# Reordering the first block of a fused attention and gated-MLP kernel: v tile by tile, q and k in one piece, norm work re-timed

## The chip, the cores and the metric

One core of a Trainium2 chip. The metric is the device time of one execution in microseconds (us). The profile names the engines PE (TensorE matmuls), PEld (TensorE weight loads), DVE (VectorE), ACT (ScalarE), POOL (GpSimd) and SP (the queue that issues transfers). Times inside a trace count from the start of the span; the span is 1.7 to 2 us shorter than the time of the same execution. L562 is line 562 of that kernel, so line numbers differ between kernels.

## The reference, cut to what matters

```python
# S = 2048 rows, D = 448, 16 heads of 28, F = 1792, all bf16
xn = layernorm(x)                                   # per row, eps 1e-5
q, k, v = split_heads(xn @ wqkv)                    # wqkv 448 x 1344
scores = q @ k.T / sqrt(28), causal, window of 256 rows
attn = softmax(scores) @ v @ wo
mlp  = (gelu(xn @ w_gate) * (xn @ w_up)) @ w_down
out  = x + attn + mlp
```

The 2048 rows are worked in four blocks of 512, each of four tiles of 128 rows. Block 0 is tiles 0 to 3, block 1 is tiles 4 to 7. 448 is three full groups of 128 contraction rows and a rest of 64. A projection is therefore three dense matmuls and one of 64 rows, and two such 64-row matmuls can run side by side on two halves of the array (in the trace of the kernel before, those of q and k both start at 10.38 us).

## The kernel before: the parts that matter

Norm, the transposing transfer, and the banks of PSUM that the projections take in turn:

```python
def norm(t):                       # VectorE: 448 columns, then the last 64 again
    xn = work.tile([P, 4, P], bf16, name="xn", bufs=4)
    for eng, lo, n, src in ((nc.vector, 0, D, 0), (nc.vector, D, 64, 384)):
        eng.tensor_scalar(out=xf[:, lo:lo + n], in0=x_sb[:, t, src:src + n], ...)
def dma_transp(t):                 # tiles 4 and up: transposed by a transfer
    nc.sync.dma_start_transpose(out=xnT[:, :, t * P:(t + 1) * P], in_=...)

ring = [("m", "m", "d"), 0]        # banks m (two buffers) and d, in turn
def bank(name):
    tag = ring[0][ring[1] % len(ring[0])]
    ring[1] += 1
    return psum.tile([P, QB], f32, name=name, tag=tag, bufs=2 if tag == "m" else 1)
```

The order of block 0, and what the three first score steps carry along for block 1 (`aux`, one entry per score step):

```python
    norm(2)
    norm(3)
    run(gen_v(0, (0,)))                       # v of tiles 0 and 1, own 64-row pair
    qk = gen_qk(0, (0,), 0, 2 * P)            # q and k of group 0, first half of the rows
    next(qk)
    transp(2, 1, nc.scalar.copy, "o")
    transp(3, 1, nc.vector.tensor_copy, "m")
    ...
    run(gen_qk(0, (0,), 2 * P, 2 * P))        # second half of the rows
    rstd(4, 2)
    ...
    aux = [lambda: rstd(6, 2), lambda: (norm(6), norm(7), loads()), lambda: None] ...
```

Of the kernel before, what the change touches and what calls it, by code (L numbers as in the profile page):

```python
# [12 lines left out]
f32 = mybir.dt.float32  # L13
i32 = mybir.dt.int32

S, D, H, Dh, F = 2048, 448, 16, 28, 1792
P = 128
NT = S // P
NF = F // P
# [56 lines left out]
def kernel(  # L76
# [21 lines left out]
    def score_pool(n):  # L98

        if phase[0] is not None:  # L100
            phase[0].close()
        phase[0] = ExitStack()
        phase[0].pool = phase[0].enter_context(tc.tile_pool(name="sps", bufs=n, space=bass.MemoryType.PSUM))

    score_pool(1)
    xv = A_x.rearrange("b (n p) d -> p (b n) d", p=P)
    outv = out.rearrange("b (n p) d -> p (b n) d", p=P)

# [12 lines left out]
    def rows(w, c0, n):  # L121
        return w[c0 * P:(c0 + n) * P, :].rearrange("(c p) n -> p c n", p=P)

    nc.sync.dma_start(out=x_sb[:, 0, :], in_=xv[:, 0, :])
    nc.scalar.dma_start(out=x_sb[:, 1, :], in_=xv[:, 1, :])
    nc.sync.dma_start(out=x_sb[:, 2:4, :], in_=xv[:, 2:4, :])
    nc.sync.dma_start(out=wv[:, 0:3, :], in_=rows(A_wqkv, 0, 3)[:, :, 2 * D:3 * D])
    nc.scalar.dma_start(out=wraw[:, 0:3, :], in_=rows(A_wqkv, 0, 3)[:, :, 0:2 * D])
    for a in range(2):
        nc.sync.dma_start(out=wv[64 * a:64 * a + 64, 3, :], in_=A_wqkv[384:448, 2 * D:3 * D])  # L130
    for a in range(2):
        nc.sync.dma_start(out=wraw[64 * a:64 * a + 64, 3, 0:D], in_=A_wqkv[384:448, a * D:(a + 1) * D])
    nc.sync.dma_start(out=x_sb[:, 4:8, :], in_=xv[:, 4:8, :])

    ident = const.tile([P, P], bf16, name="ident")
    make_identity(nc, ident[:, :])
# [16 lines left out]
                        nc.gpsimd.affine_select(out=m, in_=m, pattern=[[kind, 64]], compare_op=ALU.is_ge, fill=0.0,  # L153
                                                base=min(kind, 0), channel_multiplier=-kind)

    make_masks()

    eps_t = const.tile([P, 1], f32, name="eps_t")
    nc.vector.memset(eps_t[:, :], 1e-5)
# [15 lines left out]
    l_all = const.tile([P, NB * 4, 16], f32, name="l_all")  # L175

    def warmup(n):
        wps = phase[0].pool.tile([P, 4, QB], f32, name="wps", tag="s")
        for i in range(n):
            nc.tensor.matmul(wps[:, i % 4, :], lhsT=warm[:, 0:P], rhs=warm[:, 0:QB], start=True, stop=True)  # L180


    def stat(t):
# [11 lines left out]
    def norm(t):  # L195
        xn = work.tile([P, 4, P], bf16, name="xn", bufs=4)
        xf = xn[:, :, :].rearrange("p a b -> p (a b)")
        for eng, lo, n, src in ((nc.vector, 0, D, 0), (nc.vector, D, 64, 384)):
            eng.tensor_scalar(out=xf[:, lo:lo + n], in0=x_sb[:, t, src:src + n], scalar1=mv_all[:, t, 0:1],
                              scalar2=rstd_all[:, t:t + 1], op0=ALU.subtract, op1=ALU.mult)  # L200
        xns[t] = xn
# [27 lines left out]
# [4 lines that stand above are left out]
        return psum.tile([P, QB], f32, name=name, tag=tag, bufs=2 if tag == "m" else 1)  # L233


    def gen_v(qb, ts):

        for t in ts:
            pvs = []
            for i in range(2):  # L240
                pv = bank("pv")
                cs = slice((t + i) * P, (t + i + 1) * P)
                mm3(pv[:, 0:D], lambda c: xnT[:, c, cs], lambda c: wv[:, c, :], True, False)
                pvs.append(pv)
                yield (570, HOLD) if i else 570
            for i in range(2):
                mm_half(pvs[i][:, 0:D], xnT[:, 3, (t + i) * P:(t + i + 1) * P], wv[:, 3, :], i, False, True)
            for i in range(2):
                (nc.vector.tensor_copy if qb > 1 or i else nc.scalar.copy)(out=v_sb[:, t + i, :, 0:Dh], in_=pvs[i][:, 0:D].rearrange("p (h d) -> p h d", d=Dh))
            yield -360  # L250

    def gen_qk(qb, gs, lo=0, n=QB):

        ts = slice(qb * QB + lo, qb * QB + lo + n)
        for g in gs:
            hs = slice(4 * g, 4 * g + 4)
            pq = bank("pq")
            mm3(pq[:, 0:n], lambda c: wqp[:, c, hs, :].rearrange("p h d -> p (h d)"), lambda c: xnT[:, c, ts], True, False)
            yield 650
            pk = bank("pk")  # L260
            mm3(pk[:, 0:n], lambda c: wkp[:, c, hs, :].rearrange("p h d -> p (h d)"), lambda c: xnT[:, c, ts], True, False)
            yield 650, HOLD
            w3 = w3p[:, hs, :].rearrange("p h d -> p (h d)")
            mm_half(pq[:, 0:n], w3, xnT[:, 3, ts], 0, False, True)
            mm_half(pk[:, 0:n], w3, xnT[:, 3, ts], 1, False, True)
            nc.scalar.copy(out=qT[:, g, ts], in_=pq[:, 0:n])  # L266
            nc.vector.tensor_copy(out=kT[:, g, ts], in_=pk[:, 0:n])  # L267
            if lo + n == QB:
                done.add((qb, g))
            yield -360  # L270

    def gen_proj(qb):
# [323 lines left out]
    def run(gen):  # L596
        for _ in gen:
            pass

    warmup(10)  # L600
    stat(0)
    rstd(0, 1)
    stat(1)
    rstd(1, 1)
    norm(0)
    transp(0, 1, nc.scalar.copy, "o")
    norm(1)
    warmup(1)
    transp(1, 1, nc.scalar.copy, "d")
    stat(2)  # L610
    stat(3)
    rstd(2, 2)
    pads(nc.vector.tensor_copy, wqp, slice(0, 1))
    nc.vector.tensor_copy(out=w3p[:, :, 0:Dh], in_=wraw[:, 3, 0:D].rearrange("p (h d) -> p h d", d=Dh))
    pads(nc.scalar.copy, wkp, slice(0, 1))
    norm(2)
    norm(3)
    run(gen_v(0, (0,)))
    qk = gen_qk(0, (0,), 0, 2 * P)
    next(qk)  # L620
    transp(2, 1, nc.scalar.copy, "o")
    transp(3, 1, nc.vector.tensor_copy, "m")
    stat(4)
    run(qk)
    stat(5)
    pads(nc.vector.tensor_copy, wqp, slice(1, 4))
    pads(nc.vector.tensor_copy, wkp, slice(1, 4))
    run(gen_qk(0, (0,), 2 * P, 2 * P))
    rstd(4, 2)
    stat(6)  # L630
    v23 = gen_v(0, (2,))
    next(v23)
    next(v23)
    norm(4)
    norm(5)
    stat(7)

    def loads():

        for t in range(4, 8):  # L640
            dma_transp(t)
        nc.sync.dma_start(out=wu[:, :, :], in_=rows(B_w_up, 0, 3))
        for t3, lo, hi in ((wgu3, B_w_gate, B_w_up), (wug3, B_w_up, B_w_gate)):
            nc.sync.dma_start(out=t3[0:64, :], in_=lo[384:448, :])
            nc.sync.dma_start(out=t3[64:128, :], in_=hi[384:448, :])
        for lo in (0, F // 2):
            nc.sync.dma_start(out=wg[:, :, lo:lo + F // 2], in_=rows(B_w_gate, 0, 3)[:, :, lo:lo + F // 2])
        wo_v = A_wo.rearrange("(g j d) n -> j d g n", g=4, j=4)
        for j in range(4):
            nc.sync.dma_start(out=wo[32 * j:32 * j + Dh, :, :], in_=wo_v[j])  # L650
        for k in range(0, NF, 3):
            n = min(3, NF - k)
            nc.sync.dma_start(out=wd[:, k:k + n, :], in_=rows(B_w_down, k, n))

    for qb in range(NB):
        early = ()
        aux, plan = [], {}
        if qb < 2:
            aux = [lambda: rstd(6, 2), lambda: (norm(6), norm(7), loads()), lambda: None] * (1 - qb) + [lambda t=t: stat(t) for t in range(8, 12)] * (1 - qb) + [lambda: rstd(4 * qb + 8, 4)]
        if qb == 0:  # L660
            new_hT(0)
            early = (2, 8)
            feeds = [Feed((v23, 360), (gen_qk(0, (1, 2, 3)), 3 * QK1), (gen_proj(1), PROJ), (gen_up(0, early), UP1 * len(early)))]
            feeds[0].held = True
        else:
            ring[0] = ("m",)
            tags = "dodo" if last_tag[0] == "o" else "odod"
            feeds = [Feed((gen_down(qb - 1, tags), DOWN))]
            if qb < 3:
                feeds.append(Feed((gen_proj(qb + 1), PROJ)))  # L670
                plan = {0: 1140, 1: 1140, 2: 1300, 4: 1300, 6: 1300, 7: 1300}
            else:
                new_hT(3)
                early = (2, 4, 6, 8, 10)
                feeds.append(Feed((gen_up(3, early), UP1 * len(early))))
                plan = {0: 1300, 2: 1300, 4: 1300, 6: 1300, 7: 1300}
        if qb:
            score_pool(1)
        rest, after = attention(qb, feeds, aux, plan)
        nc.scalar.preload_act_table(ACT.Gelu_apprx_tanh)  # L680
        score_pool(2)
        if qb not in hTs:
            new_hT(qb)

        def hook(f):
            after(f)
            if f >= 4 and qb < 2:
                t = 4 * qb + 4 + f // 2
                if f < 12:
                    norm(t + 2)  # L690
                    dma_transp(t + 2)
                    if qb == 0:
                        stat(t + 6)

        gated(qb, early, rest, hook)
        if qb < NB - 1:
            nc.scalar.preload_act_table_set("natural_log_exp_and_others")
# [138 lines left out]
```

## Time and profile before

| | kernel before |
|---|---|
| time, median of 3 runs | 227.72 us (227.51 to 228.32) |
| span of the profiled execution | 225.3 us |
| PE busy | 217.1 us |
| the first scores start | 13.29 us |
| the fourth score step starts | 20.07 us |
| v of tile 7 starts | 23.44 us |
| last weight load of the kernel | 220.16 us |

The front is everything up to the fourth score step; the prediction below shows its lines. Three groups of lines are needed later and are not in it. The first is VectorE's norms of tiles 6 and 7, and SP's issue of the last of the transposing transfers (start, length, engine, line, operation, out<-in):

```profile
16.70 1.42 DVE L199 TENSOR_SCALAR xn<-x_sb,mv_all,rstd_all 128x448 bf16<-128x448 bf16 x4
...
18.93 2.32 SPq L205 DMA_TRANSPOSE xnT<-xn  x1
```

The six matmuls are the v of tiles 6 and 7 without a gap:

```profile
22.86 1.31 PE L218 MATMUL pv<-wv,xnT 128*128 128x448 bf16 x6
```

```profile
42.93 1.27 DVE L380 TENSOR_TENSOR hT<-ge,u 128x512 bf16<-128x512 bf16 x2
...
43.87 0.37 PE L223 MATMUL u<-xnT,wgu 64*128 64x512 bf16 x1
```

### The profile page before, as it was taken

The numbers are of one execution on the slowest core, as the hardware profiler recorded it, in microseconds if no ns is written. First come the engines' busy times: TensorE is split into PE (matmuls) and PEld (weight loads), VectorE is DVE, ScalarE is ACT, GpSimd is POOL, SyncE is SP. The second block draws the span as 40 slices with busy tenths as digits, with TensorE's granted clock in tenths as the row PEclk, the third lists the DMA queues.
The fourth block names the chain that finished last, engine by engine and source line by source line (L and its number), as shares of the span: only waits on it lengthen the run. The fifth ranks groups of instructions, "written<-read, shape, count | busy, mean of one in ns | idle before, by whom it ended". The sixth has DMA issues, their size and how long they took to land.

```text
span 225.3 us, 5435 instructions
## 1 busy us (share of the span) xinstructions
PE 217.1 (96%) x2262; PEld 97.0 (43%) x2262; DVE 147.6 (66%) x353; ACT 133.3 (59%) x129; POOL 43.4 (19%) x63
## 2 busy tenths in 40 slices
PE   6899999999999999999999999999999999999991
PEld 2533333344444444444444445444344435344571
DVE  5996887768675647588555666596345776679320
ACT  4678897524878876422868886333576775664000
POOL 8514867220000002222000002222000002222000
PEclk9999999999999999999999999999999999999998
DMA  6916999311100101001300100000000000100011
GB/s 222 323 28 74 314 293 292 112 23 38 36 0 24 25 5 44 4 0 37 61 0 23 25 3 25 23 0 0 0 4 20 25 5 5 43 3 0 22 42 29
DMA packets 18454, 12.69 MB, mean 56 GB/s; under 512 B 9784, under 2 KB 17784, under 8 KB 18424
## 3 DMA queue, kind: packets, MB, share of 16 engines
q1 hardware_dynamic: 17880, 11.48, 19.4%
q10 hardware_dynamic: 544, 0.80, 1.0%
q8 instruction: 19, 0.31, 0.6%
q14 instruction: 11, 0.09, 0.1%
HBM read 8.77 MB, written 1.84 MB: 47 GB/s over the span
## 4 chain that ended last, share of the span: by engine, by line
PE 87%; DVE 4%; ACT 3%; DMA 1%; POOL 1%; issue 0%; DVEq 0%
PE po L301 19%; PE gt L218 16%; PE u L218 12%; PE po L296 6%; PE sc L539 6%; PE gt L223 5%; PE ov L501 4%; PE ue L218 4%; PE pq L218 4%; PE pk L218 4%; PE pv L218 4%; PE pq L223 2%; ACT p_sb L543 1%; DMA x_sb<-in_A_x_dram 1%; POOL oN L451 1%; PE ue L223 1%
## 5 line engine op out<-in xcount | busy, mean ns | idle before, releaser
L543 ACT ACTIVATE p_sb<-sc 128x2048 bf16<-128x2048 f32 (+2 forms) x42 | 73.9, 1759 | 10.2 <-PE sc L539 8.5
L301 PE MATMUL po<-wd,hT 128*128 128x448 bf16 (+1 forms) x238 | 50.0, 342 | 0.0
L376 ACT ACTIVATE ge<-gt 128x1024 bf16<-128x1024 f32 x28 | 28.7, 1024 | 35.4 <-PE u L223 22.2
L218 PE MATMUL gt<-xnT,wg 128*128 128x512 bf16 x168 | 40.5, 380 | 0.0
L451 POOL TENSOR_TENSOR oN<-oc,rb 128x512 bf16<-128x512 f32 x10 | 12.7, 1268 | 118.0 <-DVE ri L480 62.1
L380 DVE TENSOR_TENSOR hT<-ge,u 128x512 bf16<-128x512 bf16 x42 | 26.9, 682 | 11.8 <-ACT ge L376 11.7
L218 PE MATMUL u<-xnT,wu 128*128 128x512 bf16 x126 | 30.6, 379 | 0.0
L301 PEld LDWEIGHTS <-hT 128*128 128x128 bf16 x238 | 21.6, 98 | 18.6 <-issue 2.2
L432 DVE TENSOR_TENSOR p_sb<-p_sb,masks 128x256 bf16<-128x256 bf16 (+1 forms) x90 | 24.6, 329 | 0.0
L218 PEld LDWEIGHTS <-wg 128*128 128x128 bf16 x168 | 15.1, 98 | 21.6 <-issue 5.4
L218 PEld LDWEIGHTS <-wu 128*128 128x128 bf16 x168 | 16.0, 98 | 19.2 <-issue 1.0
L507 DVE TENSOR_TENSOR oc<-oc,ov 128x512 f32<-128x512 f32 x12 | 8.3, 688 | 19.4 <-ACT oc L506 19.4
L539 PE MATMUL sc<-qT,kT 32*64 32x320 bf16 (+7 forms) x640 | 16.9, 263 | 0.5 <-ACT p_sb L543 0.3
L306 DVE TENSOR_TENSOR res<-po,x_sb 128x448 bf16<-128x448 f32 (+1 forms) x17 | 9.9, 585 | 10.4 <-PE po L301 10.1
L442 POOL TENSOR_SCALAR_AFFINE_SELECT p_sb<-p_sb 128x512 bf16<-128x512 bf16 (+1 forms) x20 | 14.2, 730 | 12.7 <-ACT p_sb L543 12.7
L296 PE MATMUL po<-wo,oN 128*128 128x448 bf16 (+1 forms) x68 | 16.3, 343 | 0.0
L267 DVE CAST kT<-pk 128x512 bf16<-128x512 f32 (+1 forms) x17 | 11.0, 649 | 7.9 <-PE pk L223 7.9
L506 ACT COPY oc<-ov 128x512 f32<-128x512 f32 x12 | 7.0, 585 | 15.2 <-POOL oN L451 12.8
L451 POOL TENSOR_TENSOR oN<-oc,l 128x512 bf16<-128x512 f32 x6 | 8.4, 1395 | 30.7 <-DVE l L468 30.7
L335 DVE CAST hT<-ue 128x512 bf16<-128x512 f32 x14 | 9.0, 686 | 7.1 <-PE ue L223 7.1
L223 PE MATMUL gt<-xnT,wgu 64*128 64x512 bf16 x49 | 13.6, 380 | 0.1
L266 ACT CAST qT<-pq 128x512 bf16<-128x512 f32 (+1 forms) x17 | 9.5, 558 | 6.6 <-PE pk L223 6.6
(75 smaller groups left out, 240.3 us busy)
## 6 DMA issues: line engine op xcount, KB each, us to landing
out_dram<-res SPq DMA_DIRECT2D x15, 112.0 KB, 1.9
wu<-in_B_w_up_dram SPq DMA_DIRECT2D x1, 1344.0 KB
wg<-in_B_w_gate_dram SPq DMA_DIRECT2D x2, 672.0 KB, 10.4
wd<-in_B_w_down_dram SPq DMA_DIRECT2D x4, 336.0 KB, 8.1
x_sb<-in_A_x_dram SPq DMA_DIRECT2D x1, 896.0 KB, 6.0
wraw<-in_A_wqkv_dram ACTq DMA_DIRECT2D x1, 672.0 KB, 4.8
x_sb<-in_A_x_dram SPq DMA_DIRECT2D x1, 448.0 KB
wo<-in_A_wo_dram SPq DMA_DIRECT2D x4, 98.0 KB
```

What stands on the lines that cost most here:

```text
L218: nc.tensor.matmul(ps, lhsT=lhs(c), rhs=rhs(c), start=start and c == 0, stop=stop and c == 2, skip_group_check=True)
L223: nc.tensor.matmul(ps, lhsT=lhs[p0:p0 + 64], rhs=rhs[p0:p0 + 64], start=start, stop=stop, tile_position=(p0, 0), skip_group_check=True)
L267: nc.vector.tensor_copy(out=kT[:, g, ts], in_=pk[:, 0:n])
L296: nc.tensor.matmul(po[:, 0:w], lhsT=oN[:, g, cs], rhs=wo[:, g, lo:up], start=(g == 0), stop=False, skip_group_check=True)
L301: nc.tensor.matmul(po[:, 0:w], lhsT=hT[:, f, cs], rhs=wd[:, f, lo:up], start=False, stop=(f == NF - 1), skip_group_check=True)
L376: nc.scalar.activation(out=ge[:, :, :], in_=pr["gt"][:, :, :], func=ACT.Gelu_apprx_tanh)
L380: nc.vector.tensor_tensor(out=hT[:, f + i, :], in0=ge[:, i, :], in1=u[:, :], op=ALU.mult)
L432: nc.vector.tensor_tensor(out=reg, in0=reg, in1=m, op=ALU.mult)
L442: nc.gpsimd.affine_select(out=reg, in_=reg, pattern=mid + [[1 if diag else -1, min(w, P)]], compare_op=ALU.is_ge, fill=0.0, base=0 if diag ...
L451: nc.gpsimd.tensor_tensor(out=oN[:, g, :], in0=oc[:, :], in1=inv, op=ALU.mult)
L539: nc.tensor.matmul(ss[k0:k0 + nk, j, col:col + nq], lhsT=kT[r, g, kt * P + k0:kt * P + k0 + nk], rhs=qT[r, g, qb * QB + q0:qb * QB + q0 + ...
L543: nc.scalar.activation(out=p_sb[:, :, 0:ncol], in_=ss[:, :, 0:ncol], func=ACT.Exp, scale=SCALE)
```

## The change

Its intent is to start v of each tile as soon as that tile is transposed, to do q and k of group 0 once over 512 columns instead of twice over 256, and to put the 64-row rests of v beside those of q and k, so that PE changes its tiling less often. Norm work of block 1 moves behind the first scores. Cut to its core:

```diff
-    score_pool(1)
+    score_pool(2)                      # q and k of group 0 borrow score banks
...
-        for eng, lo, n, src in ((nc.vector, 0, D, 0), (nc.vector, D, 64, 384)):
+        for eng, lo, n, src in ((nc.vector, 0, D, 0), (nc.gpsimd if t in (1, 2) else nc.vector, D, 64, 384)):
...                                     # gen_qk(qb, gs, others):
+            qk_halves(qb, g, pq, pk)
+            for t, pv in others:       # 64-row rests of v of tiles 2 and 3
+                v_half(t, pv)
+            if others:
+                v_copy(*others[1], nc.vector.tensor_copy)
+            qk_copies(qb, g, pq, pk)
...
-    norm(3)
-    run(gen_v(0, (0,)))
-    qk = gen_qk(0, (0,), 0, 2 * P)
-    ...
+    v_dense(0, pvs[0])
+    norm(2)
+    pads(...)                          # two on VectorE, one on ScalarE
+    transp(2, 1, nc.scalar.copy, "o")
+    pvs.append(bank("pv")[:, 0:D])
+    v_dense(1, pvs[1])
+    norm(3)
+    make_masks()
+    transp(3, 1, nc.vector.tensor_copy, "d")
+    pvs.append(alone("pv", "o"))
+    v_dense(2, pvs[2])
+    proj(pq, wqp, 0, 0)
+    proj(pk, wkp, 0, 0)
+    ...
+    pvs.append(alone("pv", "d"))
+    v_dense(3, pvs[3])
+    ring[1] = 0
...
+    def ahead():
+        for t in (4, 5):
+            norm(t)
+            dma_transp(t)
+        stat(6)
+    def ahead2():
+        stat(7)
+        rstd(6, 2)
+        v_copy(2, pvs[2], nc.vector.tensor_copy)
...
-            aux = [lambda: rstd(6, 2), lambda: (norm(6), norm(7), loads()), lambda: None] ...
+            aux = [ahead, ahead2, lambda: (norm(6), norm(7), loads())] ...
```

Cut away: the q and k weights come in four transfers, the gate weights in one, and w_down in fewer.

## The prediction

> **What bounds the kernel now.** I read the page's first lines, then busy time in three stretches, then TensorE's timeline of the front, then the chain of waits there, then VectorE's timeline. The page gives a span of 225.3 us with PE busy for 217.1 us (96%). The stretches (columns: stretch, length, then busy us and instructions of PE, PE weight loads, DVE, ACT, POOL, then clock, DMA share, GB/s) say where the rest is:
>
> ```profile
> 1.96:7.14 5.18, 4.73 (x20) 2.06 (x21) 3.77 (x14) 2.91 (x7) 4.74 (x13) 1.00 1.03 341
> 7.14:20.07 12.93, 12.09 (x81) 5.31 (x81) 11.31 (x33) 9.47 (x18) 5.46 (x13) 1.00 0.49 134
> 20.07:221.30 201.23, 200.33 (x2165) 89.65 (x2163) 131.55 (x305) 120.70 (x105) 31.89 (x32) 1.00 0.17 45
> ```
>
> From 20.07 us, where the fourth score step starts, to the end of the last matmuls PE is busy for 200.33 of 201.23 us, and the list of waits has none for PE after 18 us. That long stretch follows the front rigidly. So this change can be worth only what moves the moment at which that fourth score step starts. Before it lie 1.96 us of start-up, 5.18 us of warm-up and first norms, and 12.93 us of projections of block 0.
>
> The timeline of PE there (start, length, instruction; matmul lengths contain latency, so I use start to start):
>
> ```profile
> 7.14 1.29 PE L218 MATMUL pv<-wv,xnT 128*128 128x448 bf16 x6 [0.45 <-DMA wv<-in_A_wqkv_dram]
> ...
> 9.00 0.73 PE L213 MATMUL tp<-ident,xn 128*128 128x128 bf16 x8
> 9.96 0.49 PE L218 MATMUL pk<-xnT,wkp 128*128 128x256 bf16 x3 [0.23 <-DVE v_sb L249]
> ...
> 15.76 0.34 PE L539 MATMUL sc<-qT,kT 32*128 32x384 bf16 x4 [0.34 <-ACT p_sb L543]
> 16.24 0.81 PE L218 MATMUL pq<-xnT,wqp 128*128 128x512 bf16 x3
> ...
> 18.35 0.82 PE L218 MATMUL pq<-xnT,wqp 128*128 128x512 bf16 x3
> 19.00 0.81 PE L218 MATMUL pk<-xnT,wkp 128*128 128x512 bf16 x3
> 19.75 0.39 PE L223 MATMUL pq<-xnT,w3p 64*128 64x512 bf16 x1
> ...
> 20.07 0.40 PE L539 MATMUL sc<-qT,kT 32*128 32x128 bf16 x8
> ```
>
> Work in 7.14 to 20.07, start to start: v of tiles 0 and 1 1.52 (7.14 to 8.66), q/k group 0 in two halves 2.13 (0.34, 0.63, 1.16), two transposes 0.73, v of tiles 2 and 3 1.54, score steps 0.33, 0.28 and 0.23, three later q/k groups 1.72, 1.71, 1.72. That is 11.91, so 1.02 us is waiting: 0.23 before k at 9.96, 0.42 before the second score step at 15.76, 0.20 before q at 16.24, and the rest around 18. The chain of waits (start, length, what) says on whom:
>
> ```profile
> 13.92 1.78 ACT p_sb L543
> ...
> 15.71 0.30 ACT lnv L190
> ...
> 16.04 0.20 ACT rstd_all L191
> 16.25 0.47 ACT qT L266
> 16.72 1.36 ACT p_sb L543
> ...
> 18.12 0.29 PE sc L539 x4
> ```
>
> The single score buffer makes step two wait for the first exp; then two small ACT operations of block 1's norm (the inverse deviations of tiles 6 and 7) stand before the q copy and push the second exp to 16.7. VectorE's timeline shows that it is just as late:
>
> ```profile
> 13.84 1.09 DVE L199 TENSOR_SCALAR xn<-x_sb,mv_all,rstd_all 128x448 bf16<-128x448 bf16 x4
> 14.84 0.62 DVE L185 BATCH_NORM_STATS2 st<-x_sb 128x6 f32<-128x448 bf16 x1
> 15.50 0.18 DVE L186 BATCH_NORM_AGGREGATE mv_all<-st 128x2 f32<-128x6 f32 x1
> 15.60 0.59 DVE L249 CAST v_sb<-pv 128x448 bf16<-128x448 f32 x1
> 16.11 0.68 DVE L267 CAST kT<-pk 128x512 bf16<-128x512 f32 x1
> ```
>
> The v copy at 15.60, behind two norms and a statistic of block 1, frees the bank that q at 16.24 needs (15.60 plus 0.59 is 16.19). VectorE is busy 4.70 and 4.90 us in the two 5 us stretches from 5 to 15. It is nearly a co-bound of the front, which decides my number.
>
> **What the Trainium skill says.** "TensorEngine Tiling (Array Packing)", Tiling Modes, Key Properties, says that changing the tiling mode drains TensorE. The trace agrees: q/k of one group takes 1.72 us, six dense matmuls and a concurrent pair of 64-row ones are 7 times 0.216 = 1.51 (0.65 for three, 16.24 to 16.89), so an excursion costs about 0.2 us; for v, 1.53 against 7 times 0.19 = 1.33 (448 of 512 columns), again 0.2. "TensorE: Matmul & The Clock Gate", Part 1, says that the array runs at half clock until about 3.4 us of sustained activity, in a window that runs free of the kernel. The trace agrees: the first warm-up weight loads take 152 ns and the last 98 ns, and the turn is near 5.6 us, some 3.6 us after 1.96. "SBUF — State Buffer", SBUF: two separate sides, says that VectorE's two-port modes and GpSimd share one port pair under an exclusive lock. The trace fits that: two norms took 1.0 us with POOL idle (13.84 to 14.84) and 1.39 us while POOL masked scores (16.70 to 18.09). "DMA: Bandwidth & Descriptors", Specifications, wants at least 512 B per descriptor; the new first pieces of the q and k weights have 224 B rows. No line of this trace prices those; I take them as twice their 168 KB.
>
> **The change, part by part.**
> 1. v tile by tile, q/k in one piece, last rows shared. Two half-width q/k groups (2.13) become one: 7 times 0.216 plus one excursion is 1.72, saving 0.41. The v of tiles 0 to 3 lose two excursions of their own, since their last rows ride in group 0's and group 1's: 3.06 becomes 4 times 0.57 plus two pairs of 0.19, or 2.66, saving 0.40. Work falls from 11.91 to about 11.1.
> 2. The q/k weights in four pieces (the heads of group 0 first) instead of one. Before, wv was on the path: PE waited 0.45 us for it at 7.14, behind 672 KB of q/k weights. Now 168 KB of them precede it, so at the 375 GB/s of that stretch I estimate it near 6.4. But a statistic now stands ahead of the second norm, which ends near 6.6 instead of 6.0 (0.65 us more on VectorE), and its transposes near 7.05. The first v starts at 7.05: gain 0.1.
> 3. My time table from there, with durations of this trace: third norm 7.35 to 7.75, transposes to 8.15, v of tile 1 to 8.75, transposes of tile 3 to 9.15, v of tile 2 to 9.75 (its copy on ACT, behind the fourth deviation and the k padding, is done near 9.1), q and k to 11.1, four half-row matmuls to 11.6, v of tile 3 to 12.3. Meanwhile the copies of q (ACT 0.57) and k (DVE 0.6) end near 12.1. So the first scores start at about 12.3 instead of 13.29. Gain here 1.0, of which 0.19 is owed for the last rows of tiles 2 and 3.
> 4. First exp 12.7 to 14.55 (1.88 before). q/k group 1 with the v rows ends near 14.4, the second scores run 14.6 to 14.9. So 0.42 us of waiting shrinks to about 0.15, and the two ACT operations of tiles 6 and 7 come after the second exp.
> 5. Then VectorE: k copy to 12.0, two small pads to 12.4, v of tile 1 to 12.9, two larger pads to 13.5, norms 4 and 5 to 14.5, one statistic to 15.25, v of tile 3 to 15.8. The next q needs that bank. PE is ready at 14.9, so a new wait of 0.9 us appears (0.20 before). The masks of POOL now run until about 13.3 (6.0 us from 7.2) beside those pads; allow 0.1 to 0.4 for the shared port. I take 15.9.
> 6. From there to the fourth scores: 0.65 and 1.07 for group 2, 0.3 scores, 1.72 group 3, as before, to about 19.65.
>
> Sum: 20.07 minus 19.65 is 0.4 us, of about 0.8 us less work and 1.0 us at the first scores; the rest is given back at the bank of step 5. 227.72 minus 0.4 is 227.3 us.
>
> What is off the path: fewer, larger loads of later weights (gate weights in one piece; they are read at 39.4, and 3.7 MB from 22.9 at 300 GB/s end near 35), eight warm-ups for ten, masks later (needed first in block 1), two 64-column norm tails on POOL.
>
> **The rivals.**
> - Without the VectorE wait. If the v copy comes by 14.9 (for it: one statistic, 0.75, and two tails less are ahead of it), PE has only 0.3 to 0.4 us of waits: 7.05 plus 11.1 plus 0.4 is 18.55, a gain of 1.5 and a time of 226.2. Against it: the k copy cannot start before the half rows end near 11.4, and the seven operations of step 5 then follow.
> - The start slips. The second norm comes later, the short rows load slowly, POOL's tails wait for the port, or eight warm-ups with a thinner sequel leave the array at half clock for another window. Every 0.5 us of delay at the first v is 0.5 us more; half clock over part of the v work some 1.5. Time 227.8 to 229. For it speaks that the turn to full clock came only near 5.6; against, that PE still has work from 1.96 to 6.2.
> - A later wait. Norms 6 and 7 now come after two v copies, some 1.1 us later (19.2 for 18.1). The transpose of tile 7 started moving 1.1 us after its issue and took 1.0, so it lands near 22.4; its v is due at 22.9. Another 1 us late on VectorE costs 0.5 us: 227.8.
>
> **Range and chances.** All waits gone gives 226.2, all gain lost and a slip gives 228; within, VectorE decides. 8 in 10: 226.4 to 228.0. Two per cent is 4.6 us, more than all waiting of the front, so faster by that has chance 0.01; slower by it would need the clock and a load to fail together, 0.02; within 0.97.
>
> **What would show it.** Right: the first scores near 12.3, second near 14.6; PE's longest wait after 10 us before group 2's q, put down to the v copy, near 1 us; fourth scores near 19.6; no PE waits afterwards. Wrong: the first v after 7.5; weight loads of 152 ns past 6.5 us; a wait at the v of tile 7 or at a gate matmul; or group 2's q starting right after the second scores.

## More of the kernel before

The gated part (its code and its lines at 43 us are in this section) takes up the turn of the banks where the attention left it, for its first pair only. The later pairs have a turn of their own between "d" and "o":

```python
def begin(f):                                  # f = 0, then pairs (2, 4), (6, 8), ...
    ...
    tags = (("m", 2), alone)                   # alone: "d" or "o", by turns
    if qb == 0 and f == 0:
        nxt = [ring[0][(ring[1] + i) % 3] for i in range(2)]
        tags = [(x, 2 if x == "m" else 1) for x in nxt]
```

## The result, and the profile after

| | before | after |
|---|---|---|
| time, median of 4 runs each | 227.95 us (227.51 to 228.32) | 228.74 us (228.45 to 228.87) |
| ratio after/before, fast runs | | 1.0034, 95% interval 1.0011 to 1.0056 |
| span of the profiled execution | 225.3 us | 227.0 us |
| PE busy | 217.1 us | 215.0 us |

Ratios here are the mean time of one kernel's fast runs over that of the other's fast runs of the same rounds, so they are not quite the ratio of the medians quoted. One execution of the kernel before, beside four of the experiments (from the v copy on ScalarE to the norm tails on VectorE), was slow (313.76 us at a clock of 0.658) and is left out.

The change is within 2%, as predicted, but on the other side: 0.8 us slower where 0.4 us faster was expected, and outside the range. PE shows 2.1 us less busy time and ends later. But 25 of the 2,252 matmul records are missing from this trace. In the repeat below, whose trace has them all, PE is busy for 217.0 us, so nearly all of the 2.1 us is missing records and not saved work. The stretches of the new kernel, with the columns as in the prediction, are these:

```profile
6.85:19.94 13.09, 11.52 (x75) 4.29 (x75) 12.04 (x34) 9.15 (x17) 8.66 (x25) 1.00 0.54 159
19.94:222.50 202.56, 198.75 (x2141) 89.42 (x2163) 131.52 (x305) 120.69 (x105) 32.12 (x32) 1.00 0.18 45
```

PE was busy for 200.33 of 201.23 us in the long stretch before. It now shows 198.75 of 202.56, with 22 records missing there. The repeat, with none missing, shows 200.64 of 202.14 (from 19.71 us): 1.50 us not busy for 0.90 before. (All three windows end 1.1 us behind the last weight load.) The front is ahead only by 0.13 us at its end, in this pair of profiles. PE's timeline there:

```profile
6.85 0.73 PE L221 MATMUL pv<-wv,xnT 128*128 128x448 bf16 x3
...
12.49 0.40 PE L562 MATMUL sc<-qT,kT 32*128 32x128 bf16 x8
...
16.28 0.81 PE L221 MATMUL pq<-xnT,wqp 128*128 128x512 bf16 x3 [1.02 <-DVE v_sb L246]
...
19.94 0.40 PE L562 MATMUL sc<-qT,kT 32*128 32x128 bf16 x8
```

The first scores come 0.80 us sooner than before. Then q of group 2 waits 1.02 us for VectorE's v copy, as foreseen. VectorE has the norms of tiles 4 and 5 and a statistic ahead of that copy, and then another statistic, another copy and a k copy ahead of the norms of tiles 6 and 7:

```profile
15.64 0.59 DVE L246 CAST v_sb<-pv 128x448 bf16<-128x448 f32 x1
16.15 0.68 DVE L274 CAST kT<-pk 128x512 bf16<-128x512 f32 x1
16.75 0.62 DVE L188 BATCH_NORM_STATS2 st<-x_sb 128x6 f32<-128x448 bf16 x1
...
17.49 0.59 DVE L246 CAST v_sb<-pv 128x448 bf16<-128x448 f32 x1
18.13 0.69 DVE L274 CAST kT<-pk 128x512 bf16<-128x512 f32 x1
18.74 1.11 DVE L202 TENSOR_SCALAR xn<-x_sb,mv_all,rstd_all 128x448 bf16<-128x448 bf16 x4
```

The norms that started at 16.70 now start at 18.74. SP's issues of the two transposing transfers that hang on them, the chain of waits there, and PE where it needs tile 7 (the kernel after):

```profile
19.36 2.17 SPq L208 DMA_TRANSPOSE xnT<-xn  x1
...
21.63 1.22 SPq L208 DMA_TRANSPOSE xnT<-xn  x1
```

```profile
21.63 2.42 DMA xnT<-xn
24.05 0.05 issue
```

```profile
24.10 0.74 PE L221 MATMUL pv<-wv,xnT 128*128 128x448 bf16 x3 [0.62 <-DMA xnT<-xn]
```

The first v of tile 7 starts 0.65 us later than before, 24.10 for 23.44. And in the gated part of block 0 a wait appears where there was none (VectorE's two multiplications, and the second 64-row matmul of the pair after):

```profile
43.50 1.28 DVE L403 TENSOR_TENSOR hT<-ge,u 128x512 bf16<-128x512 bf16 x2
```

```profile
44.83 0.37 PE L226 MATMUL u<-xnT,wgu 64*128 64x512 bf16 x1 [0.29 <-DVE hT L403]
```

The matmul at 44.83 starts right as the second multiplication ends at 44.78. The list of waits of PE is a check that these are the large ones after the start-up (line, releaser, us in all, times, longest). Left out of it here are 0.8 us in five pieces at gate matmuls, put down to "issue". They have no counterpart in the repeat, whose records are complete:

```profile
PE pq L221 <- DVE v_sb L246: 1.0, 1, 1.0
...
PE pv L221 <- DMA xnT<-xn: 0.6, 1, 0.6
PE u L226 <- DVE hT L403: 0.3, 1, 0.3
```

### The profile page after: what moved, and what is told of

It is laid out like the page before. It is cut to its first block, busy times and chain, and to the rows that moved or that the text cites. A ratio compares the mean times of both kernels' runs of the same rounds, so it can differ in the third digit from the quotient of the medians.

```text
span 227.0 us, 5398 instructions
## 1 busy us (share of the span) xinstructions
PE 215.0 (95%) x2227; PEld 95.4 (42%) x2252; DVE 148.0 (65%) x353; ACT 132.9 (59%) x129; POOL 44.3 (20%) x65
## 4 chain that ended last, share of the span: by engine, by line
PE 77%; DVE 9%; DMA 4%; POOL 2%; ACT 2%; issue 2%; SPq 2%; DVEq 0%
PE po L324 16%; PE gt L221 14%; PE u L221 10%; PE po L319 5%; PE sc L562 5%; PE gt L226 4%; PE ue L221 4%; PE pq L221 4%; PE ov L524 4%; PE pk L221 3%; PE pv L221 3%; POOL oN L474 2%; PE pq L226 2%; DMA oc<-ri 1%; DVE st L188 1%
## 5 line engine op out<-in xcount | busy, mean ns | idle before, releaser
L221 PE MATMUL gt<-xnT,wg 128*128 128x512 bf16 x162 | 39.3, 380 | 1.0 <-issue 0.8
L403 DVE TENSOR_TENSOR hT<-ge,u 128x512 bf16<-128x512 bf16 x42 | 26.9, 683 | 12.1 <-ACT ge L399 11.9
L221 PEld LDWEIGHTS <-wu 128*128 128x128 bf16 x168 | 16.0, 98 | 19.2 <-issue 1.0
L274 DVE CAST kT<-pk 128x512 bf16<-128x512 f32 x15 | 10.2, 682 | 6.6 <-PE pk L226 6.6
L221 PE MATMUL pq<-xnT,wqp 128*128 128x512 bf16 x36 | 11.7, 380 | 1.5 <-DVE v_sb L246 1.0
```

The source lines that it names most:

```text
L221: nc.tensor.matmul(ps, lhsT=lhs(c), rhs=rhs(c), start=start and c == 0, stop=stop and c == 2, skip_group_check=True)
L274: nc.vector.tensor_copy(out=kT[:, g, ts], in_=pk)
L403: nc.vector.tensor_tensor(out=hT[:, f + i, :], in0=ge[:, i, :], in1=u[:, :], op=ALU.mult)
```

## A ruler for small differences

The same program varies by half a microsecond from one execution to the next, so spans of single profiles decide nothing here. I used marks instead. The last 2,187 weight loads of PE come in the same order in both kernels, so the start of a given load can be compared. (A weight load can start 0.01 us ahead of its matmul, hence 19.93 here and 19.94 above.) The lengths between marks repeat to 0.02 us, except where something waits and except from m to g. These are marks and lengths read from the traces (s4 and s6 are the fourth and the sixth score step; m is a score step of block 1 behind the gated part of block 0; g is a gate matmul of block 1; e is the last weight load):

```
kernel                    s4   s4 to s6  s6 to m  m to g  g to e
before                 20.07     4.42     45.56   18.71   131.42
before, second profile 20.55     4.41     45.55   18.93   131.44
after                  19.93     5.13     45.93   19.02   131.39
after, second profile  19.71     4.69     45.93   19.04   131.38
```

Three things are read from it. From s4 to s6 the new kernel loses 0.27 to 0.71 us: that is tile 7. From s6 to m it loses 0.37 us both times: that is the wait at 44.83. From m to g it differs by 0.3 in the first pair of profiles, but the second profile of the kernel before has most of that too, so it belongs to the execution and not to the change (over all 16 profiles it lies between 18.70 and 19.34, in either kernel).

The second profiles also show the front fairly: s4 is 20.07 and 20.55 before (20.39 and 20.33 in two variants with an unchanged front), and 19.93, 19.71, 19.71, 19.70 and 19.76 in the five profiles of the new front. The first profile of the kernel before was its quickest. On average the new front is 0.57 us ahead (20.34 less 19.76).

## The experiments

Theory: two things outside the front take its gain back, (1) the transposing transfer of tile 7, late because the norms of tiles 6 and 7 are late, and (2) a bank of PSUM, because the new line `ring[1] = 0` shifts the turn of the banks, which the first pair of the gated part takes over. Rivals: the loss is chance of the execution; it is the slower front itself (GpSimd and VectorE in each other's way); or the late stretch differs for some other reason.

### Unedited, once more

The kernel after, without an edit.

> The changed kernel unedited, for its spread. Its profile ended 1.7 us after that of the kernel before, of which TensorE lost 0.71 at the v of tile 7, 0.38 at the second up projection of block 4 of the first gated part, 0.31 at 88.7 us, and 0.45 after the last matmul; it won 0.13 before. If all is built in, the ratio stays near 1.0075; if the 0.31 and the 0.45 are chance of one execution, as I think, near 1.004 (+0.8 to +1.0 us), with both first waits again in the profile (0.6 to 0.9 and 0.3 to 0.5).

228.34 us (227.87 to 228.82); the kernel before on that chip 227.88 us; ratio 1.0016 (0.9999 to 1.0032). Both waits are there again, at tile 7 with 0.27 us in place of 0.71. So the loss is 0.4 to 0.8 us (by this run alone it can't be told from zero), and its bank part is steady. Both the ratio and the wait at tile 7 are below what was expected.

### The norms of tiles 6 and 7 one score step sooner

```diff
-  aux = [ahead, ahead2, lambda: (norm(6), norm(7), loads())] ...
+  aux = [ahead, lambda: (ahead2(), norm(6), norm(7), loads()), lambda: None] ...
```

> Changed kernel with norms and transposes of tiles 6 and 7 in the second score step, not the third. Theory 1 (the late norm, then the transposing transfer, holds the v of tile 7): norm 7 ends near 19.2 instead of 19.85, the transfer lands 0.6 to 1.5 us earlier, the wait of 0.7 us shrinks below 0.2, time falls by 0.5 to 0.7 us against the changed kernel. Rival (the transfer itself is slow, by an instruction fetch on the same rings): the landing moves by 0.6 at most and a wait of 0.2 or more stays; time falls under 0.4. Wait for a bank at 44 us unchanged in both.

227.98 us, ratio 1.0000 (0.9986 to 1.0013). Tile 7 landed at 22.93 instead of 23.38, s4 to s6 is 4.42 as before, and no wait is left there. The bank wait stays (45.93). The median fell by 0.36 us and not by 0.5 to 0.7: in time this agrees with the rival (a slow transfer) as well, and it is the trace, with no wait left, that speaks for the theory. The transfer was slow here too (see "One rule for all runs").

### The turn of the banks restored

```diff
   for f in fs:                      # gen_up
+      if qb == 0 and f == 8:
+          ring[1] += 2
```

The counter counts while the program is built, not on the chip. It stands at 30 in the kernel before when the gated part begins, and at 22 in the new one (24 if it weren't reset): modulo 3, 0 and 1. With 0 the first pair takes banks m and m, with 1 it takes m and d, and the second pair to want bank d is the one at 44.83. Two more make 24.

> Changed kernel with the counter of PSUM banks set on by two before the second early up projection, so that the first gated pair has the two banks that it has in the kernel before. Theory 2 (resetting that counter put the second up projection of the first gated pair into the bank that the third pair needs): the wait of 0.3 to 0.4 us at 44 to 45 us goes, time falls by 0.3 to 0.4 us; the wait at the v of tile 7 stays. Rival (the wait at 44 us is VectorE being late since 24 us): it stays, time unchanged.

227.73 us, ratio 0.9999 (0.9983 to 1.0015). s6 to m is 45.56, exactly as before; the wait at tile 7 stays (4.69). In time neither repair by itself is told from the unedited kernel by the intervals; the lengths between marks tell them apart.

### Both

> Both edits. If the two waits are all that turned the gain at the front into a loss: 0.9 to 1.1 us below the changed kernel, and 0.0 to 0.3 us below the kernel before (ratio 0.9985 to 1.000). If something else slows the rest of the kernel (fewer, larger loads; masks later), it stays above the kernel before by 0.2 us or more.

227.83 us (226.85 to 228.34), ratio 0.9983 (0.9965 to 1.0001). Its middle is the predicted gain (0.4 of 227.7 us is 0.9982), but the interval reaches from none to twice that. It lies wholly below that of the result (1.0011 to 1.0056), so the two repairs together are seen in time. The step from the repeat is 0.75 us by the ratios, where 0.9 to 1.1 was expected. Its profile fell on one of its slower executions and still has 0.36 us at tile 7; s6 to m is 45.56.

### The v copy of tile 3 on ScalarE

On top of the two repairs, the wait of 1.02 us that the prediction named:

```diff
-                v_copy(*others[1], nc.vector.tensor_copy)
+                v_copy(*others[1], nc.scalar.copy)
```

> Both mendings, and the v copy of tile 3 on ScalarE, ahead of its q copy, instead of VectorE. Theory (VectorE's queue, with norms 4 and 5 and a statistic ahead of that copy, holds the q matmul of group 2 by 1.0 us): the q matmul starts near 15.3 instead of 16.1, fourth scores near 19.2, which is 0.9 us before those of the kernel before; part of it may come back as a wait for tile 7 (0 to 0.7). Time 0.2 to 0.9 us below the run with both mendings, ratio to the kernel before 0.995 to 0.998. Rival (ScalarE becomes the bound: its second exp moves later by the copy): fourth scores not before 19.6, time as with both mendings.

227.36 us (227.01 to 227.72) beside 228.20 us for the fast runs of the kernel before; ratio 0.9971 (0.9951 to 0.9992), the first that is surely faster. PE in this variant, at q of group 2 and at v of tile 7:

```profile
15.33 0.81 PE L221 MATMUL pq<-xnT,wqp 128*128 128x512 bf16 x3 [0.20 <-ACT v_sb L246]
...
23.18 0.74 PE L221 MATMUL pv<-wv,xnT 128*128 128x448 bf16 x3 [0.31 <-DMA xnT<-xn]
```

q starts 0.95 us sooner than in the kernel after, the fourth score step at 19.25. The wait at tile 7 is back, though: v is due sooner and the transfer is not.

### Into the kernel before: late norms, and the other bank

Two edits of the kernel before, one each, to see whether a single cause makes it slower:

```diff
-  aux = [lambda: rstd(6, 2), lambda: (norm(6), norm(7), loads()), lambda: None] ...
+  aux = [lambda: rstd(6, 2), lambda: None, lambda: (norm(6), norm(7), loads())] ...
```

> The kernel before, with norms and transposes of tiles 6 and 7 one score step later. If the late norm is enough by itself: norm 7 ends near 19.5 to 20, a wait of 0.3 to 1 us appears before the v of tile 7, time 0.2 to 0.9 us up. If the transfers have slack in this kernel: no wait, time unchanged.

228.37 us, ratio 1.0004 (0.9982 to 1.0026): no loss. Tile 7 landed at 23.79, 1.3 us later than in the kernel before, yet s4 to s6 is 4.42. The late norm alone is not enough: with the old front, v of tile 7 is due at that very moment. But this is also the one profile of 14 in which neither issue of the two transfers was stretched (see below), so it doesn't show what a late norm with a stretched issue would cost this kernel.

```diff
-      nxt = [ring[0][(ring[1] + i) % 3] for i in range(2)]
+      nxt = ["m", "d"]
```

> The kernel before, with the second up projection of the first gated pair put into the other bank, as the reset counter does. If the bank clash is enough by itself: a wait of 0.3 to 0.4 us at the second up projection of the third pair, near 44 us, and time 0.3 to 0.4 us up (ratio 1.0013 to 1.0018). If not: no change.

228.44 us, ratio 1.0021 (0.9998 to 1.0044). s6 to m is 46.10, so 0.54 us are lost, but not as I had thought: the bank d still held the projection before it, and the first pair itself waited (0.40 us at 39.4, for VectorE's copy of that bank). It shows that this place has no slack. It doesn't repeat the wait at 44.83, so the proof of cause 2 is the repair above, not this.

### The two norm tails back on VectorE

On top of the two repairs, `nc.gpsimd if t in (1, 2) else nc.vector` becomes `nc.vector`.

> Both mendings, and the two 64-column norm tails back from GpSimd to VectorE; the masks then start at 3.6 us again. If the tails on GpSimd cost more than they save (two VectorE copies at 7.6 took 0.89 and 0.82 us instead of 0.25 and 0.28): third norm's end and the fourth transposes come 0.1 to 0.3 us earlier, but VectorE has 0.4 us more to do, so at the bank wait of 16.1 nothing is won: time within 0.2 us of the run with both mendings. If they are a real help: 0.3 us or more slower.

227.44 us, ratio 0.9974 (0.9954 to 0.9995). The first scores start at 12.30, the fourth step at 19.70, just as with the tails on GpSimd (12.31 and 19.76). The tails on GpSimd gain nothing that shows. In the kernel after two paddings of weights took 0.89 and 0.82 us while GpSimd ran a tail and then the clearing of the masks (VectorE, then GpSimd):

```profile
7.58 0.89 DVE L617 COPY wqp<-wraw 128x336 bf16<-128x336 bf16 x1
7.76 0.82 DVE L644 COPY w3p<-wraw 128x448 bf16<-128x448 bf16 x1
```

```profile
7.14 0.61 POOL L202 TENSOR_SCALAR xn<-x_sb,mv_all,rstd_all 128x64 bf16<-128x64 bf16 x1 [0.84 <-ACT rstd_all L194]
7.66 0.74 POOL L151 MEMSET masks<- 128x768 bf16 x1
```

With the tails on VectorE they took 0.27 and 0.26 us. But they did so too in two of the profiles with the tails on GpSimd (the unedited repeat and the run with the banks restored), and first scores came at 12.30 there, at 12.27 and 12.31 in two profiles with long paddings. So this collision comes and goes, and costs the first scores nothing that shows.

### The kernel before, once more

> The kernel before, unedited, a second profile of it: this measures how far the same program's front moves from one execution to the next. My theory says that its wait for the v weights at the first v (0.45 us in the first profile, 1.0 and about 0.2 in two variants with the same front) is chance, so first v between 6.9 and 7.9 us, fourth scores between 19.9 and 20.6 us. Rival: the front is fixed within 0.1 us and the ratio of the changed kernel is all in its program; then the fourth scores are at 20.0 to 20.1 again. Time ratio 1.000 within 0.002 either way.

227.86 us, ratio 0.9994 (0.9976 to 1.0013). The first v starts at 7.5 instead of 7.14 and s4 is 20.55: the same program's front moves by half a microsecond. That is the rival "chance of the execution", measured. It is as large as the whole effect in one profile, and it doesn't touch the lengths s4 to s6 and s6 to m.

### Tails on VectorE and the copy on ScalarE together

> The variant with norms 6 and 7 earlier, the bank turn restored and the v copy of tile 3 on ScalarE, with the two norm tails also back on VectorE. Each of the two last steps alone was 0.3% faster than the kernel before. If tails on GpSimd bring nothing and cost nothing (theory), this equals the variant without it within 0.2 us, 227.4, ratio 0.997. Rival: both gains are real and independent; then 0.9945, about 226.8 us.

227.24 us (226.72 to 227.72), ratio 0.9966 (0.9949 to 0.9984), like the copy alone (0.9971). The front shows the most extreme case (PE, fourth score step and v of tile 7):

```profile
18.89 0.40 PE L564 MATMUL sc<-qT,kT 32*128 32x128 bf16 x8
...
23.19 0.74 PE L221 MATMUL pv<-wv,xnT 128*128 128x448 bf16 x3 [0.66 <-DMA xnT<-xn]
```

The fourth step is 1.18 us ahead of the kernel before, v of tile 7 starts 0.26 us ahead of it. All of the further gain of the front goes into the wait for the transfer.

### The paddings of group 0's weights behind the third norm

The three `pads` lines move from before the transposes of tile 2 to just before those of tile 3, on the variant with ScalarE's copy; in the second run the tails are on VectorE as well.

> The ScalarE-copy variant with the three paddings of group 0's weights moved behind the third norm. Theory: two of them took 0.85 us instead of 0.25 because GpSimd held the shared port, and they delay norm 3 to 8.5 us; out of its way norm 3 ends about 0.4 us earlier, the fourth transposes start near 8.5 instead of 8.9, first scores near 12.0 instead of 12.4, and time falls 0.3 us to about 227.1 (ratio 0.9955). Rival: the paddings then hold up q of group 0, which needs them at about 9.8 us; then first scores stay at 12.4 or later and the time stays at 227.4. Second rival: the gain is taken back as a wait for tile 7's transposing transfer.

227.09 us (226.63 to 228.01), ratio 0.9964 (0.9945 to 0.9984).

> The same with the two norm tails back on VectorE. If the GpSimd tails are what holds the port, the paddings and norm 3 now take their short lengths (0.25 us and about 0.4 us) and first scores come near 11.9; if masks alone hold it, no difference from the run before. Time 227.0 to 227.3 us, ratio 0.995 to 0.997.

226.78 us (226.62 to 227.85), ratio 0.9949 (0.9935 to 0.9964). From the first v to the first scores it takes 5.25 and 5.12 us, against 5.43 and 5.38 in the same variants with the paddings where they were. But the five profiles of the new front as it was (the kernel after, its repeat, the two repairs and both) spread from 5.24 to 5.64, so a gain of the order isn't shown. The first scores start at 12.04 as expected, and at 12.21 in the second run where 11.9 was expected. In time the two can't be told from the run before by their intervals. The last of them has the lowest median, 1.1 us below the kernel before on that chip.

### Tile 7 transposed by TensorE

What was open by then: whether the transfer alone takes the front's gain back, or another wait would stand behind it. Tile 7 is transposed by four matmuls ahead of v of tile 4, and not by a transfer:

```diff
+            if t == 4:                                      # gen_v
+                transp(7, 1, nc.vector.tensor_copy, ring[0][ring[1] % 3])
+                ring[1] += 1
-        for t in (6, 7):                                    # loads
-            dma_transp(t)
+        dma_transp(6)
```

(The restored turn then needs one more instead of two.) It was put on the variant with copy and tails, and on the one with the paddings moved too.

> The variant with ScalarE's v copy and the tails on VectorE, and tile 7 of block 1 transposed by TensorE (4 transposes, about 0.28 us of its time, and a copy of 0.43 us on VectorE) instead of by a transfer. If the transfer alone takes the gain back (theory), no wait at the v of tile 7, the lead over the kernel before behind it is 1.0 to 1.1 minus 0.28, that is 0.7 to 0.8 us instead of 0.32, and the time falls by 0.4 us to about 226.8. Rival: another wait takes its place (the copy on VectorE, the q of block 1, the exp chain); then the lead at the next scores is again 0.3 to 0.4 us and the time 227.2 or more.

227.16 us, ratio 0.9960 (0.9936 to 0.9983). PE has no wait of that kind any more:

```profile
19.54 0.38 PE L216 MATMUL tp<-ident,xn 128*128 128x128 bf16 x4
...
22.21 1.31 PE L221 MATMUL pv<-wv,xnT 128*128 128x448 bf16 x6
```

The lead over the kernel before at s6 is 0.64 us (23.84 for 24.48), twice the 0.32 us of the same kernel with the transfer, and it is 0.37 us at the last weight load, where that kernel has none left. (Both lose some from m to g, where the first profile of the kernel before was the quickest of all 16.) s4 to s6 is 4.76: the 4.42 and 0.34 us of transposing. So up to s6 nothing else waits behind the transfer. The median fell by less than 0.1 us, where I expected 0.4: in time the step is not resolved.

> The same edit on the variant with the paddings behind norm 3 and the tails on VectorE (0.53 us ahead behind the v of tile 7, wait 0.33 us there). Wait gone, 0.28 us more work: theory gives a lead of 0.55 to 0.65, so almost nothing in time, 226.7 to 226.9. Rival as above: lead under 0.3 and time 227.0 or more.

227.00 us, ratio 0.9951 (0.9929 to 0.9974), as its twin with the transfer (0.9949). Lead at s6 0.71 us; here the transfer had cost 0.50 us and TensorE's transposes cost 0.35. The lead is what the theory gave, and the time (226.7 to 226.9 expected) is at the edge of the rival's 227.0.

### One rule for all runs

In the kernel before, v of tile 7 would start 3.40 us after s4 if nothing waited (4.42 from s4 to s6, less the 1.02 from the landing of a late tile 7 to s6, which is 25.07 less 24.05 in the kernel after). What a run loses should then be its landing less (s4 + 3.40), where that is positive. Landings are from the trace; the loss is s4 to s6 less 4.42:

```
run                       s4    landing  landing-(s4+3.40)  loss
before                  20.07    22.46        -1.01         0.00
before, late norms      20.39    23.79         0.00         0.00
after                   19.93    24.05         0.72         0.71
after, once more        19.71    23.38         0.27         0.27
norms sooner            19.71    22.93        -0.18         0.00
banks restored          19.70    23.38         0.28         0.27
both                    19.76    23.52         0.36         0.36
both, tails on VectorE  19.70    22.82        -0.28        -0.01
both, copy on ScalarE   19.25    23.13         0.48         0.48
copy and tails          18.89    23.14         0.85         0.85
paddings moved          18.95    22.88         0.53         0.52
paddings and tails      19.04    22.94         0.50         0.50
```

The rule was fitted on one row and holds in the others to 0.01 us. In the rows with a loss it is bookkeeping, and what it checks is that nothing else waits between s4 and s6. It says what the front is worth: a quicker front moves s4, the landing follows VectorE and the queue, and the later of the two sets v of tile 7.

The landing has a part that doesn't come from the norms. An undisturbed issue of a transposing transfer takes 1.2 us, and it lands 2.42 us after its start. In all eight rows with a loss, one of the two issues is stretched, to 1.73 to 2.40 us. Taking the excess off (an estimate from the traces), tile 7 would have landed 0.25 to 0.72 us before it was due in every one of them: in the kernel after at 24.05 less 0.97, or 23.08, with v due at 23.33. So a loss takes both, a landing with little slack (late norms, or a quicker front) and a stretched issue. The kernel before had a stretch of 1.1 us too and absorbed it with 1.01 us to spare. No run removed the stretch, so its own cause stays open (a correlation stands in the last section).

## Why the prediction was wrong, point by point

- The front was right at its end. First v 7.05 predicted, 6.85 measured; first scores 12.3, measured 12.49, and 12.27 to 12.31 in the four others with the same front; the wait of q of group 2 0.9, measured 1.02, put down to the v copy; fourth scores 19.65, measured 19.93 here and 19.70 to 19.76 in the others. The first two rivals (no wait on VectorE; a slipping start or half clock) did not come about: no weight load of about 150 ns starts after 5.7 us in the kernel after.
- The parts of that gain were not those predicted, so that its end agrees is in part luck. The first v starts at 7.40 us on average in the four profiles with the front of the kernel before, and at 6.83 in the five of the new front: 0.57 us sooner, where 0.1 was predicted. From there to the fourth scores it takes 12.93 us on average in both. So at the fourth scores the new order of the projections had given back all that it had gained (0.6 us at the first scores, counted from the first v), and the whole lead came from the earlier start (the 0.45 us wait for the v weights at the first v is gone). With ScalarE's copy, where the wait before q of group 2 is short, the same stretch takes 12.33 us (6.92 to 19.25).
- The step that failed is the one from the front to the end: "That long stretch follows the front rigidly. So this change can be worth only what moves the moment at which that fourth score step starts." It was read from a profile in which no PE wait was left after 18 us. But that shows only that other things were in time with the old order, and the change moved two of them. The prediction's own signs of being wrong name the first, "a wait at the v of tile 7"; the second showed at an up projection, which they don't name.
- The first is the transfer of tile 7. The prediction has it under "A later wait", as a rival, with a landing near 22.4 and v due at 22.9. The mechanism was right and its size was off. Due: 19.93 and 3.40 is 23.33. Landing: 24.05, and 23.38 in the repeat. The norms ended at 19.85 and not at 19.2, since the v copies came later and a k copy also stands ahead of them. And the 3.2 us that the prediction allows from norm to landing hold for undisturbed issues only (tile 6's issue at 19.36, 1.2 us, then 2.42 us for tile 7); the stretch of tile 6's issue to 2.17 us made them 4.20. That term could have been read in the kernel before, where the norms end at 18.13 and tile 7 lands at 22.46, 4.33 us later: with it, 19.2 gives 23.5, behind a v due at 23.05 (19.65 and 3.40; the prediction has 22.9), that is a wait of about 0.5 us, more than the whole predicted gain. (From the issue of tile 7 to its landing the prediction reads 1.1 and 1.0 us; in that trace it is 18.93 to 22.46, or 3.53 us.)
- The second is the bank. Under "What is off the path" the prediction has nothing on the turn of the banks, although the diff shows `ring[1] = 0`. The counter reset at the v of tile 3 (11.79 us in the kernel after) sets the banks of the gated part (from 38.48 us). It cost 0.37 us in each of the three profiles that had the shifted turn (after, its repeat, norms sooner), and 0.00 in every one of the new front with the turn restored.
- In the sum: the front brought 0.13 us in the profiles shown and 0.57 on average, tile 7 took 0.27 to 0.71, the bank 0.37. That is a net loss of 0.1 to 0.5 us, where 0.4 to 0.8 us were measured, so some 0.3 us are not in this sum (the last point here may hold a part of them). With both repaired the ratio is 0.9983, what was predicted for the change; with this sum and that interval the close agreement is in part luck.
- Not settled: the time from the last weight load to the end of the span is 5.1 to 5.7 us in the four profiles with the front of the kernel before, and 5.3 to 5.8 in the six with the new front on which nothing but banks, norm timing and tails was varied. That may be 0.2 us of the change or chance; no run tells it apart.

## What to carry to other kernels

A long stretch without waits is not rigid: it shows that everything arrived in time for the old order, so for each thing it needs write down when it lands and when it is due, and do it again for the new order, before counting what a faster front is worth. Take the time from cause to landing from a trace, with its stretched cases, and not from the undisturbed one. Look in the diff for shared counters, turns and buffers that are read long after the changed lines. For effects below the spread of the whole, compare lengths between corresponding instructions, and take a second profile of the unchanged kernel before calling a difference a cause.

## What the Trainium skill lacked or had wrong

- "Runtime: NRT & Kernel Launch", Instruction fetch mechanics, says that an engine's instructions are refilled in blocks of 16 KiB over a DMA queue, and that the cost is "mostly hidden". Between 10 and 26 us each trace shows one 16,384-byte instruction packet; it takes 0.9 to 1.5 us and starts between 18.7 and 20.1 us. Of 14 profiles with tiles 6 and 7 transposed by transfers, 13 have one of the two issues stretched to 1.73 to 2.40 us, each time one that the packet overlapped, and the other at 1.19 to 1.22 us. In the fourteenth (late norms in the kernel before) the packet overlapped an issue by 0.7 us, and both took 1.2 us. This is a correlation; no run moved the packet alone. In the kernel after, the stretched issue was tile 6's, which delayed tile 7's as well; in the kernel before it was only the last one.
- "DMA: Bandwidth & Descriptors" has no duration, from issue to landing, for a transposing transfer of one 128x512 tile inside SBUF on this chip. Here: 1.2 us for the issue, which holds its queue, and 2.4 us from the start of an undisturbed issue to the landing (21.63 to 24.05 us in the kernel after), 3.3 us where the issue was stretched to 2.17 us (19.36 to 22.64).
- "SBUF — State Buffer", SBUF: two separate sides, speaks of an exclusive lock between VectorE's two-port modes and GpSimd, and excepts no GpSimd operation from it. The paddings of 0.27 us that took 0.89 us fit that. But in the kernel before (7.56 and 7.87 us) and in the profiles with the tails on VectorE, GpSimd ran mask selections through the same time, and the paddings took 0.25 to 0.28 us. So either not every GpSimd operation holds VectorE up, or these paddings don't need the shared port (and the 0.89 us have another cause); no run here tells which.
